# Four low parts of the output weights as a product on ScalarE and a subtraction on GpSimd, with the first 450 words of the order around them

## The chip, the cores and the metric

The kernel runs on one core of one Trainium2 chip. A core has five engines with a queue each: TensorE (PE, matrix products), VectorE (DVE), ScalarE (ACT), GpSimd (POOL) and SyncE (SP, which here only issues DMA transfers). Each engine takes its instructions strictly in the order in which the program holds them, and waits at a semaphore where an operand isn't there yet. The metric is the device time of the whole program in microseconds (us), as the median of several runs; smaller is better.

## The reference, cut to what matters

```python
def _attn_ref(q, k, v):                    # 8 batches, 8 heads, 576 positions, 64 per head
    scores = q @ k.transpose / 8           # masked: a band of 32, or every 4th of a band of 128
    attn = softmax(where(masks, scores, -1e9))
    return attn @ v

def _moe_ref(x, w_in, w_out, g_ln):        # x: 4608 x 512, w_in: 512 x 1024, w_out: 1024 x 512
    h = x @ w_in
    sm = softmax(h)                        # over the 1024 columns
    solu = h * sm
    ln = (solu - mean(solu)) / sqrt(var(solu) + 1e-6) * g_ln
    return ln @ w_out
```

The weights and `g_ln` come as 64-bit floats. The kernel reads their bits and makes 32-bit values of them, and it multiplies `g_ln` into the rows of `w_out`.

## The kernel before

**Attention** works in 32 units (n = 0 to 31; a unit is two heads of one batch). A unit goes through these steps, each a *word* of the program: `q` and `v` load its queries, keys and values (SP); `S` makes its scores in PSUM (PE); from unit 6 on `mask` adds the mask (DVE), before that PE does; `max` (DVE); `sub` (DVE up to unit 5, then POOL); `exp` (ACT); `sum` and `inv` (DVE); `norm` (POOL or DVE, by the table `POOL_NORM`); `turn` transposes (DVE); `V` multiplies by the values into PSUM (PE); `xh` and `xc` copy the result out (ACT), and `xl` forms the part below it (DVE or POOL).

**The second layer** works in 36 tiles of 128 rows. Products are in 32-bit words cut into a high and a low part, three products for one. For tiles 0 to 9 the words `hp hq hr hs` (columns 0 to 511) and `ht hu hv hw` (columns 512 to 1023) each make a quarter of one half of `h`, which is three matmuls; `ha hb hc hd` each make two such quarters. Then come `peak` (DVE), `e` (ACT), `gate` (DVE), `mid` (subtracts the mean; ACT or DVE by the table `ACT_CENTRE`), `var` (ACT, and six short steps on POOL), `forth` and `back` (through DRAM, SP), `trA trB` (DVE), `thA thB` (ACT), `tlA tlB` (POOL or DVE) and `o` (PE, 24 matmuls: the product with `w_out`).

**The weights** are 16 blocks of 128 x 512 (b = 0 to 7 are `w_in`, 8 to 15 are `w_out`). For each block `w` loads it (two DMAs of 256 KB), `field` and `low` cut out its bits (ACT), `sign` its sign (ACT if the block is in `ZERO_SIGN`, else DVE), `join` puts them together (DVE), `hi` writes the high part (ACT) and `lo` the low part. Blocks 8 to 15 take in `g_ln` on the way, in one of two forms:

```python
    def conv_gain(b):                                        # line 917, ACT
        cv[b]["gained"] = True
        nc.scalar.activation(out=cv[b]["mag"], in_=cv[b]["mag"], func=AF.Copy, scale=gain(b))
    def conv_lo(b):                                          # lines 929 to 935
        if b < 8 or "gained" in cv[b]:
            eng = nc.vector if b in DVE_LOW else nc.gpsimd
            eng.tensor_tensor(out=out, in0=mag, in1=high, op=ALU.subtract)
        else:
            nc.vector.scalar_tensor_tensor(out=out, in0=mag, scalar=gain(b), in1=high,
                                           op0=ALU.mult, op1=ALU.subtract)
```

Without the word `gain` both `hi` (line 925) and `lo` (line 933) multiply by `g_ln` themselves, and `lo` is on VectorE. With it `hi` is a plain cast (line 923) and `lo` a plain subtraction (line 931). Before the change only block 13 has the word.

**What sets the order.** The text `OPENING` is a list of some 1,200 words. The kernel goes through it once, from left to right, and each word writes its instructions at the end of its engine's queue; nothing sorts them later. So a word's place decides what it stands behind on its own engine, SP's loads among them, and the semaphores do the rest.

**What is shared.** The eight 2 KB banks of PSUM hold everything PE writes: tiles 0, 2, 4 use banks 0 and 1, the tiles between them banks 2 and 3, the scores of units 0 to 3 lie in banks 2 and 3, those of later units in banks 5 and 6, and `V` writes to parts of banks 4 to 7. The regions of `V` and of later `S` are tracked as overlapping, so a `V` waits for whoever still reads the `S` that stands ahead of it in the list, and the other way round. The weights' 64-bit words lie in seven buffers by the table `SLOTS`; block 7 takes that of block 0, block 10 that of block 3, and so on.

Of the kernel before, what the change touches and what calls it, by code (L numbers as in the profile page):

```python
# [42 lines left out]
POOL_NORM = (0, 1, 2, 4, 5, 6, 7, 8, 10, 11, 12, 15, 18, 21, 22)  # L43
ACT_SCORES = ()
POOL_X = (2, 4, 5, 6, 9)
DVE_LOW = (1, 4, 8, 9, 10, 11, 12, 14, 15)
ACT_CENTRE = (0, 3, 4, 5, 6, 8, 9, 10, 11, 13, 14, 15, 17, 19, 20, 21)
# [3 lines left out]
ZERO_SIGN = (2, 3, 5, 6, 7, 9, 11, 12, 13, 15)  # L51
OPENING = (
# [1044 lines left out]
```

## Time and profile before

| | us |
|---|---|
| median of 3 runs | 479.35 (479.26 to 479.41) |
| the profiled execution's own time | 478.46 |
| its span, first to last instruction | 476.7 |
| PE busy in the span | 455.9 (96%) |
| DVE, ACT, POOL busy | 351.3, 296.3, 274.9 |

The span is that of one execution, the times are those of others: a difference that is worked out on the span's clock is carried over to the median as it is. PE's busy time counts a matmul from its start to its modelled end. Where a row of the profile ends in square brackets, the engine stood idle before the instruction, for so many us, and what follows the arrow ended that.

### The profile page before, as it was taken

The page shows a single profiled execution, that of the slowest core. Times are in us where ns is not written, and L with a number is a line of the kernel's source. Part 1 is how long each engine was busy: PE and PEld are TensorE (multiplying, and loading weights), DVE is VectorE, ACT ScalarE, POOL GpSimd, SP SyncE. Part 2 cuts the span into 40 slices and gives each one's busy share as a digit, 9 for nine tenths or more (in the row PEclk, how much of TensorE's full clock was granted, in tenths as well). Part 3 has the DMA queues.
Part 4 walks back from the last instruction along what each step waited for, and adds up shares of the span by engine and source line. Part 5 has one row for each costly group of instructions (what it writes and reads, how often), then busy time and mean ns, then how long its engine had stood idle before and what let it go on. Part 6 is the DMA issues. An engine that isn't in the chain of part 4 may idle for free.

```text
span 476.7 us, 15670 instructions
## 1 busy us (share of the span) xinstructions
PE 455.9 (96%) x6590; PEld 369.5 (78%) x6590; DVE 351.3 (74%) x640; ACT 296.3 (62%) x502; POOL 274.9 (58%) x340
## 2 busy tenths in 40 slices
PE   2689999999999999999999999999999999999996
PEld 1467777888888888888788888888888888888885
DVE  3878899999989497788698948768584845446472
ACT  4687997754456636644755663647585847667452
POOL 0453666654587797985384434647575755656320
PEclk9999999999999999999999999999999999999999
DMA  8999895758647647665677846564854745453461
GB/s 259 321 325 327 271 285 151 209 183 259 210 133 210 173 142 214 195 208 190 176 217 196 258 133 192 151 224 140 286 151 130 204 139 137 130 154 112 110 194 70
DMA packets 56661, 92.57 MB, mean 194 GB/s; under 512 B 6288, under 2 KB 32400, under 8 KB 56592
## 3 DMA queue, kind: packets, MB, share of 16 engines
q1 hardware_dynamic: 55872, 90.93, 62.7%
q8 instruction: 51, 0.84, 0.7%
q10 hardware_dynamic: 720, 0.66, 0.4%
q14 instruction: 18, 0.15, 0.1%
HBM read 58.53 MB, written 28.31 MB: 182 GB/s over the span
## 4 chain that ended last, share of the span: by engine, by line
PE 50%; DVE 1%; issue 0%; ACT 0%; ACTq 0%; DVEq 0%
PE banks L605 24%; PE banks L834 19%; PE banks L406 3%; PE banks L640 2%; PE banks L321 2%; DVE tl L596 0%; DVE t L510 0%; DVE sm L345 0%; DVE pt L390 0%; DVE t L858 0%; ACT ob L654 0%; DVE mu L521 0%; DVE t L522 0%; ACTq L654 0%; DVEq L345 0%
## 5 line engine op out<-in xcount | busy, mean ns | idle before, releaser
L605 PE MATMUL banks<-w_o,th 128*128 128x512 f32 x544 | 168.9, 391 | 0.0
L605 PEld LDWEIGHTS banks<-w_o,th 128*128 128x128 f32 x544 | 101.3, 188 | 21.6 <-DVE mu L510 0.2
L605 PE MATMUL banks<-w_o,tl 128*128 128x512 f32 x272 | 106.0, 390 | 0.0
L596 POOL TENSOR_TENSOR tl<-t,th 128x512 fp32r<-128x512 f32 x36 | 49.7, 1386 | 35.7 <-ACT th L590 33.8
L858 DVE CUSTOM_DVE_ANT_0 t<-banks,t 128x512 f32<-128x512 f32 x39 | 26.6, 688 | 45.9 <-PE banks L834 40.4
L605 PEld LDWEIGHTS banks<-w_o,tl 128*128 128x128 f32 x272 | 51.0, 188 | 10.9
L590 ACT CAST th<-t 128x512 fp32r<-128x512 f32 x68 | 41.0, 617 | 20.9 <-DVE t L582 15.4
L475 PE MATMUL banks<-w_i,x_hi 128*128 128x512 f32 x160 | 52.3, 409 | 0.8 <-DVE mu L510 0.8
L366 POOL TENSOR_TENSOR sm<-sm,mx 128x576 f32<-128x576 f32 x26 | 32.5, 1254 | 28.5 <-DVE mx L353 28.5
L582 DVE STREAM_TRANSPOSE t<-raw 128x512 f32<-128x512 f32 x68 | 46.0, 693 | 1.7 <-DMA raw<-mid 1.5
L321 PE MATMUL banks<-kt,qt 64*32 64x64 f32 x2304 | 34.2, 235 | 13.7 <-DMA qt<-qT 7.4
L321 PEld LDWEIGHTS banks<-kt,qt 64*32 64x32 f32 x2304 | 27.8, 111 | 23.8 <-issue 13.6
L510 DVE CUSTOM_DVE_ANT_0 t<-t,e 128x1024 f32<-128x1024 f32 x25 | 32.0, 1280 | 15.2 <-ACT e L501 15.1
L406 PEld LDWEIGHTS banks<-pt,vt 32*64 32x64 f32 x2624 | 33.7, 135 | 10.9 <-issue 2.6
L501 ACT ACTIVATE e<-t,nmax 128x1024 f32<-128x1024 f32 x25 | 28.8, 1150 | 20.8 <-DVE nmax L865 20.6
L852 ACT COPY t<-banks 128x512 f32<-128x512 f32 x39 | 22.6, 586 | 30.5 <-PE banks L834 21.2
L526 ACT ACTIVATE e<-t 128x1024 f32<-128x1024 f32 x35 | 37.0, 1058 | 6.0 <-DVE t L522 5.7
L617 ACT ACTIVATE ob<-banks,rstd 128x512 f32<-128x512 f32 x35 | 23.9, 684 | 25.0 <-PE banks L605 15.6
L406 PE MATMUL banks<-pt,vt 32*64 32x64 f32 (+1 forms) x2624 | 37.2, 235 | 2.1 <-ACT x_hi L444 1.0
L519 ACT ACTIVATE t<-t,mu 128x1024 f32<-128x1024 f32 x22 | 25.3, 1152 | 16.7 <-DVE mu L518 11.4
L385 POOL TENSOR_TENSOR sm<-sm,rs 128x576 f32<-128x576 f32 x15 | 18.9, 1259 | 28.5 <-DVE rs L380 27.9
L475 PEld LDWEIGHTS banks<-w_i,x_hi 128*128 128x128 f32 x160 | 29.1, 191 | 7.5 <-DVE mu L510 1.3
(162 smaller groups left out, 959.0 us busy)
## 6 DMA issues: line engine op xcount, KB each, us to landing
mid<-t SPq DMA_DIRECT2D x140, 128.0 KB, 2.6
raw<-mid SPq DMA_DIRECT2D x34, 512.0 KB, 3.8
out<-ob SPq DMA_DIRECT2D x35, 256.0 KB, 3.0
vt<-vw SPq DMA_DIRECT2D x24, 352.0 KB, 4.9
kt<-kT SPq DMA_DIRECT2D x24, 304.0 KB, 4.3
qt<-qT SPq DMA_DIRECT2D x24, 288.0 KB, 4.5
x_hi<-x SPq DMA_DIRECT2D x12, 288.0 KB, 3.8
t<-w_in SPq DMA_DIRECT2D x10, 256.0 KB, 4.6
```

What stands on the lines that cost most here:

```text
L321: nc.tensor.matmul(out=ps[WIN * g : WIN * g + WIN, WQ * s0 : WQ * s0 + WQ], lhsT=qt[D * h : D * h + D, q0 : q0 + WIN], rhs=kt[D * h : D * ...
L366: eng.tensor_tensor(out=st[n]["sm"], in0=st[n]["sm"], in1=wide(mx), op=ALU.subtract)
L406: nc.tensor.matmul(out=ps_x[D * h : D * h + D, r // 2, c0 : c0 + k1 - k0], lhsT=vt[WIN * g : WIN * g + WIN, slot, :], rhs=pt[WIN * g : WIN ...
L475: nc.tensor.matmul(out=ps_h(i)[:, half], lhsT=a[:, kt, xs], rhs=w_i[:, kt, half, part, :], start=(kt == 0 and k == 0), stop=(kt == KT - 1 ...
L501: nc.scalar.activation(out=e, in_=h, func=AF.Exp, bias=nmax, scale=1.0, accum_out=se)
L510: nc.vector.tensor_tensor_reduce(out=t, in0=h, in1=ms[i]["e"], scale=1.0, scalar=0.0, op0=ALU.mult, op1=ALU.add, accum_out=mu,)
L526: nc.scalar.activation(out=e, in_=t, func=AF.Square, accum_out=per_tile(i, "sq"))
L582: nc.vector.transpose(out=turned(i)[:, cut(c)].rearrange("p k (a r) -> p k a r", r=WIN), in_=ms[i]["mv"].rearrange("p (a k s) -> p k a s", ...
L590: nc.scalar.copy(out=ms[i]["th"][:, cut(c)], in_=turned(i)[:, cut(c)])
L596: (nc.gpsimd if on_pool else nc.vector).tensor_tensor(out=ms[i]["tl"][:, cut(c)], in0=turned(i)[:, cut(c)], in1=ms[i]["th"][:, cut(c)].bit ...
L605: nc.tensor.matmul(out=ps_o(i), lhsT=a[:, f, :], rhs=w_o[:, f, part, :], start=(f == 0 and k == 0), stop=(f == FT - 1 and k == 2), skip_gr ...
L834: nc.tensor.matmul(out=banks[:, bank], lhsT=left(pa, kt), rhs=right(pb, kt), start=j in (1, 2, 5) and kt == 0 and k == 0, stop=kt == 1 and ...
```

## The change

Blocks 11, 12, 14 and 15 get the word `gain`, and none of them stands in `DVE_LOW` any more: `g_ln` is multiplied in on ACT, `hi` becomes a cast, and `lo` a subtraction on POOL in place of one VectorE operation. Beside this five tables change, and the first 450 or so words of `OPENING` stand in another order; the rest of it, from `fa1 tlA4 out3 gate7` on, is the same.

```diff
-POOL_NORM = (0, 1, 2, 4, 5, 6, 7, 8, 10, 11, 12, 15, 18, 21, 22)
+POOL_NORM = (0, 1, 4, 5, 6, 7, 10, 11, 12, 15, 18, 21, 22)
-DVE_LOW = (1, 4, 8, 9, 10, 11, 12, 14, 15)
-ACT_CENTRE = (0, 3, 4, 5, 6, 8, 9, 10, 11, 13, 14, 15, 17, 19, 20, 21)
+DVE_LOW = (3, 6, 8, 9, 10)
+ACT_CENTRE = (0, 1, 4, 5, 6, 8, 9, 10, 11, 13, 14, 15, 17, 19, 20, 21)
-ZERO_SIGN = (2, 3, 5, 6, 7, 9, 11, 12, 13, 15)
+ZERO_SIGN = (0, 2, 3, 5, 8, 9, 12, 13, 15)
...
-    "exp3 v2 xl1 w4 ht0 low4 sign4 V2 field4 field6 lo5 hi3 xh2 ht1 xc2 join4 hi4 q5 S5 lo3 w7 "
...
+    "hi3 sub3 exp3 lo2 field6 ht0 lo3 V2 w7 field7 sum3 w10 sign4 xc2 xh2 join6 low7 hq0 inv3 "
+    "norm3 hp1 turn3 field4 sign7 q5 w8 hi6 low10 S5 v3 V3 ht1 join4 hi4 xh3 lo5 q4 lo6 field10 "
...
```

So the low parts of blocks 1 and 4 go from VectorE to POOL and those of 3 and 6 the other way; `norm` of units 2 and 8 goes from POOL to VectorE; `mid` of tile 1 goes from VectorE to ACT and that of tile 3 the other way; of the signs VectorE has seven in place of six and ACT nine in place of ten.

**The loads, on SP's queue, from block 6 on.** `tp` is block 6, `vt_469` (after: `vt_458`) the values of unit 2, `raw` block 4, `kt_537` and `qt_536` (after: `kt_556`, `qt_555`) keys and queries of unit 5, `t<-w_in` block 7, the first `t<-w_out` block 9 (after: 10), the second block 8, and `vt_609` (after: `vt_605`) the values of unit 3. Before:

```order
L258 DMA tp<-w_in 128x512 x2
L258 DMA vt_469<-vw 128x320
L258 DMA vt_469<-vw 128x384
L258 DMA raw_473<-w_in 128x512 x2
L258 DMA kt_537<-kT 128x304 x2
L258 DMA qt_536<-qT 128x288 x2
L258 DMA t_581<-w_in 128x512 x2
L258 DMA t_601<-w_out 128x512 x2
L258 DMA vt_609<-vw 128x320
L258 DMA vt_609<-vw 128x384
L258 DMA t_612<-w_out 128x512 x2
```

And after:

```order
L258 DMA tp<-w_in 128x512 x2
L258 DMA vt_458<-vw 128x320
L258 DMA vt_458<-vw 128x384
L258 DMA raw_467<-w_in 128x512 x2
L258 DMA t_525<-w_in 128x512 x2
L258 DMA t_532<-w_out 128x512 x2
L258 DMA kt_556<-kT 128x304 x2
L258 DMA qt_555<-qT 128x288 x2
L258 DMA t_561<-w_out 128x512 x2
L258 DMA vt_605<-vw 128x320
L258 DMA vt_605<-vw 128x384
```

The queries of unit 5 moved behind two more weight blocks, and the values of unit 3 behind one more.

**VectorE around the softmax of unit 5.** L390 is `turn3`, L353 and L363 on `banks` are `max5` and `sub5`, L461 is `xl3`, L912 a `join`, L931 a `lo`, L904 a `sign`, L374 `sum5`. Before, with the semaphores that each waits for:

```order
L390 STREAM_TRANSPOSE pt_596<-sm_95 128x576 [waits DVE_49]
L353 TENSOR_REDUCE mx<-banks 128x9 [waits PE_49,Activation_49]
L363 TENSOR_TENSOR sm_95<-banks,mx 128x9x64 [waits DVE_49]
L912 SCALAR_TENSOR_TENSOR mag_594<-mag_594,low_585 128x512 [waits Activation_49]
L931 TENSOR_TENSOR w_i<-mag_522,w_i 128x512
L904 TENSOR_SCALAR low_625<-t_612 128x512 [waits DMAHW1_49,DMAHW0_49,Activation_49]
L374 TENSOR_REDUCE rs<-sm_95 128x9 [waits Activation_49]
L461 TENSOR_TENSOR x_lo<-banks,x_hi 128x576 [waits Activation_49]
```

And after:

```order
L390 STREAM_TRANSPOSE pt_550<-sm_95 128x576 [waits DVE_49]
L904 TENSOR_SCALAR low_540<-t_525 128x512 [waits DMAHW7_49,DMAHW6_49,Activation_49]
L912 SCALAR_TENSOR_TENSOR mag_552<-mag_552,low_470 128x512 [waits Activation_49]
L931 TENSOR_TENSOR w_i<-mag_479,w_i 128x512 [waits Activation_49]
L904 TENSOR_SCALAR low_565<-t_532 128x512 [waits DMAHW1_49,DMAHW0_49,Activation_49]
L353 TENSOR_REDUCE mx<-banks 128x9 [waits Activation_49]
L363 TENSOR_TENSOR sm_95<-banks,mx 128x9x64 [waits DVE_49]
L461 TENSOR_TENSOR x_lo<-banks,x_hi 128x576
```

`V3` now stands right behind `S5` in the list and ahead of `max5`. So `V3` no longer waits for `sub5`, and `max5` waits for ACT's count at `xh3`, the copy that follows `V3`.

## Rows read from the trace of the kernel before

**Rows 1.** Busy time by stretch: PE, PEld, DVE, ACT, POOL; then PEclk, DMA, GB/s

```profile
30.00:40.00 10.00, 8.08 (x247) 6.12 (x246) 7.76 (x14) 8.39 (x15) 5.81 (x4) 1.00 0.98 322
30.00:70.00 40.00, 36.20 (x876) 28.05 (x875) 35.83 (x60) 35.48 (x60) 24.34 (x31) 1.00 0.94 297
70.00:220.00 150.00, 150.00 (x2460) 122.47 (x2459) 129.24 (x218) 87.14 (x145) 107.86 (x134) 1.00 0.62 191
```

**Rows 2.** Timeline of PE: start, us, instruction, idle before and its end

```profile
28.15 1.20 PE L406 MATMUL banks<-pt,vt 32*64 32x32 f32 x80
...
31.29 0.79 PE L321 MATMUL banks<-kt,qt 64*32 64x64 f32 x48 [1.05 <-ACT x L448]
32.95 0.43 PE L321 MATMUL banks<-kt,qt 64*32 64x64 f32 x24 [0.86 <-issue]
...
35.73 1.13 PE L406 MATMUL banks<-pt,vt 32*64 32x32 f32 x80
...
55.89 1.13 PE L406 MATMUL banks<-pt,vt 32*64 32x32 f32 x84 [1.01 <-ACT x_hi L444]
...
63.87 0.62 PE L475 MATMUL banks<-w_i,x_hi 128*128 128x512 f32 x2
...
69.27 0.73 PE L475 MATMUL banks<-w_i,x_hi 128*128 128x512 f32 x2 [0.57 <-DVE mu L510]
...
79.82 0.67 PE L605 MATMUL banks<-w_o,th 128*128 128x512 f32 x2
```

**Rows 3.** SP's issues: unit 5's queries, block 9, unit 3's values, each with its landing

```profile
23.88 1.02 SPq L258 DMA_DIRECT2D qt<-qT  x2
...
DMA to landing us min/median/max: 4.6/4.8/4.9
...
26.96 0.97 SPq L258 DMA_DIRECT2D t<-w_out  x2
...
DMA to landing us min/median/max: 4.2/4.8/5.4
...
27.99 0.89 SPq L258 DMA_DIRECT2D vt<-vw  x2
...
DMA to landing us min/median/max: 5.5/5.5/5.6
```

**Rows 4.** Timeline of VectorE, columns as in the timeline of PE

```profile
37.87 0.76 DVE L461 TENSOR_TENSOR x_lo<-banks,x_hi 128x576 fp32r<-128x576 f32 x1 [0.27 <-ACT x_hi L444]
39.62 0.47 DVE L904 TENSOR_SCALAR low<-t 128x512 uint16<-128x512 uint16 x1 [0.99 <-ACT low L891]
...
52.99 0.76 DVE L374 TENSOR_REDUCE rs<-sm 128x9 f32<-128x585 f32 x1 [1.50 <-ACT sm L370]
...
62.22 1.23 DVE L510 CUSTOM_DVE_ANT_0 t<-banks,e 128x1024 f32<-128x1024 f32 x1
...
86.61 0.76 DVE L345 TENSOR_TENSOR sm<-banks,dilated 128x576 f32<-128x576 f32 x1
```

**Rows 5.** Groups by line and form, 0 to 130 us: count, busy, mean ns, idle before

```profile
L385 POOL TENSOR_TENSOR sm<-sm,rs 128x576 f32<-128x576 f32 x11 | 13.8, 1256 | 28.5 <-DVE rs L380 27.9 <-ACT e L501 0.5
L931 POOL TENSOR_TENSOR w_i<-mag,w_i 128x512 fp32r<-128x512 f32 x6 | 7.7, 1297 | 9.1 <-ACT w_i L923 9.1
L933 DVE SCALAR_TENSOR_TENSOR w_o<-mag,packed,w_o 128x512 fp32r<-128x512 f32 x7 | 5.2, 738 | 0.0
L522 DVE TENSOR_SCALAR t<-t,mu 128x1024 f32<-128x1024 f32 x3 | 2.3, 754 | 0.1
L931 POOL TENSOR_TENSOR w_o<-mag,w_o 128x512 fp32r<-128x512 f32 x1 | 1.4, 1417 | 0.0
L919 ACT ACTIVATE mag<-mag,packed 128x512 f32<-128x512 f32 x1 | 0.7, 708 | 0.0
```

**Rows 6.** Timeline of VectorE and of POOL around one `norm`

```profile
40.68 0.64 DVE L912 SCALAR_TENSOR_TENSOR mag<-mag,low 128x512 int32<-128x512 int32 x1
...
40.86 1.49 POOL L385 TENSOR_TENSOR sm<-sm,rs 128x576 f32<-128x576 f32 x1 [2.18 <-DVE rs L380]
```

143 rows, old and new, of the table OPENING are left out of this document.

## The prediction

> **What bounds the kernel now.** I read the busy time by stretch first. From 70 to 220 us PE is busy for 150.00 of 150.00 us, while VectorE is busy for 129.24, ACT for 87.14 and POOL for 107.86 [rows 1]: there no other engine's work can be worth anything, as long as it isn't late. PE stands still ahead of that: between 30 and 70 us it is busy for 36.20 of 40 [rows 1], so 3.8 us are to be had there. The change edits exactly this part, and PE's matmuls are the same before and after. So the question is a single one: at what time does PE begin `o0`, the first product with `w_out` (79.82 now [rows 2]), with the same work behind it? At that point all of units 0 to 10's `S`, units 0 to 7's `V` and all of tiles 0 to 5's `h` are done in both orders, so a shift of `o0` is a shift of the end.
>
> The timeline of PE names the stops: 1.05 us ahead of `S5`, 0.86 inside it, 1.01 ahead of `V5`, 0.57 ahead of `hc5` [rows 2]. VectorE is nearly as full: 35.83 of these 40 us [rows 1], with two stops of its own, 0.99 and 1.50 us [rows 4].
>
> **The low parts themselves.** VectorE loses four fused operations: 4 x 0.738 = 2.95 us [rows 5]. ACT gains four products of 0.708, 2.8 us [rows 5], and POOL four subtractions of 1.297 (`w_i`) to 1.417 (`w_o`), 5.2 to 5.7 us [rows 5]. With the tables beside it: `norm2` and `norm8` put 2 x 0.76 = 1.5 us on VectorE (at the 0.76 of `xl3`, a step of the same size [rows 4]) and take 2 x 1.256 = 2.5 us off POOL [rows 5]; one more sign costs VectorE 0.47 (as the one at 39.62 [rows 4]); `lo1`, `lo4` against `lo3`, `lo6`, and `mid1` against `mid3`, change engines one for one. In sum VectorE does 1.0 us less, POOL 2.7 to 3.2 more, ACT some 2 more. Nothing of this is on PE's path by itself. What hides POOL's share: it is idle for 15.7 of the 40 us from 30 to 70 [rows 1], and the four parts are wanted only from the fourth quarter of `o0` on. Uncovered, it would cost up to the whole 5.7.
>
> **The loads.** SP's queue is issued in order, and the DMA engines are busy for 0.98 of 30 to 40 us at 322 GB/s [rows 1]; so what lands when is a matter of how many bytes stand ahead. Unit 5's second half of queries is issued at 24.57 and lands at 29.2 (24.57 + 4.6 [rows 3]). After, blocks 7 and 10 stand ahead of it: 2 x 524 KB at 322 GB/s are 3.3 us more, so it lands at about 32.5. Unit 3's values land at 34.0 now (28.5 + 5.5 [rows 3]), and stand behind one block more: 34.0 + 1.6 = 35.6; I take 35.5.
>
> **PE up to `V3`.** What stands ahead of `S5` is ready as now: `V2` started at 28.15 [rows 2], and after it come two quarters in place of one, to about 30.7. `S5` then waits for its queries until 32.5 to 33 (31.29 now). The stop of 0.86 in its middle is put down to "issue", time in which PE waits for nothing that the profile shows [rows 2]; I take it as gone, since PE has stood still for 2 us just ahead of it, and as 0.86 at most if not. `S5` ends at about 34, ahead of the values of unit 3 either way, so this does not count. `V3` follows it directly now and starts with those values at 35.5, against 35.73 [rows 2]; it ends at about 36.55 against 36.86. But by then PE has done four quarters (`hp0 ht0 hq0 hp1`) where it had done six. A quarter is three matmuls, 0.69 us from start to start, so PE is 1.4 us of work behind and 0.3 us of time ahead: **1.1 us behind**.
>
> **VectorE from there.** `max5` waits for the copy `xh3` behind `V3`, and everything behind it on VectorE waits too: `sub5`, `xl3`, `join7`, and so on to the `gate` steps. VectorE has run out of work at about 34.8, so it stands still for some 2.4 us. With 0.7 us for the copy (between 0.6 and the 1.0 that lie between the end of `V3` and `xl3` now, 37.87 - 36.86 [rows 2, 4]) `max5` starts at 37.25; it, `sub5` and `xl3` take 2.1 together, to 39.35. Now `xl3` ends at 38.63 and `gate2` at 63.45 [rows 4]: 24.82 us, of which 0.99 and 1.50 are stops, so 22.33 of work. After, the list between the two holds `join7` (0.64), `sum5` (0.76), `sign11` (0.47), `fa0` and `trA0` (at the 0.64 of a `join`) and an `inv` (0.2) more, a sign (0.47) and the VectorE half of `mid1` (0.754 [rows 5]) less: +2.1, or 24.5. I find no stop in it: `exp5`, `exp6`, `e0` to `e2` on ACT and `norm4` to `norm6` on POOL each come ahead of their reader, by 0.1 to 1.5 us. So `gate2` ends at 63.85 and `ha4` starts at 63.95, against 63.87 [rows 2]. The 1.1 us that PE was behind are made up on the way, because the stop of 1.01 ahead of `V5` shrinks to what PE needs to catch up.
>
> **From `ha4` to `o0`** PE's work is the same 15.4 us in both. Now 0.57 of waiting for `gate3` come on top; after, `hc5` stands four quarters later and finds it done. In its place `hb4` waits for `xl7`, which is late by about 0.2. So `o0` starts at 79.82 + 0.1 - 0.57 + 0.2 = 79.55, **0.3 us earlier**. In `o0` the low parts of blocks 11, 12 and 15 are wanted 2, 2.7 and 4.8 us after its start; POOL has them at about 71, 80.5 and 83.3, so the last has 1 us to spare. Behind `o0` stands `V8`, which waits for unit 10's `mask` on VectorE. Its end is 87.37 now [rows 4]; after, VectorE has 1.0 us less to do up to there, 0.7 us of later start, and 2.5 us of stops less, and ends at about 84.6, when `o0` ends at 85.0.
>
> The forecast is therefore 479.35 - 0.3, or **479.0 us** (the execution profiled: 478.46 - 0.3).
>
> **A rule that speaks against it.** The `norm` at 40.86 took 1.49 us [rows 6], where eleven of its kind take 1.256 in the mean [rows 5]. It began inside a VectorE `join`, which reads two operands of SBUF and ended at 41.32, 0.46 us later. The Trainium skill ("SBUF — State Buffer", section "Who interferes with whom") says that a VectorE instruction with two SBUF inputs and a GpSimd instruction that reads SBUF exclude each other on a shared port, and that whichever issues second waits. These rows agree with it. By it the four new subtractions would cost VectorE up to their own length each where they come first, as an estimate 5.7 us at the most; by the row, 0.23 each, 0.9 us in all, and that is spread over both engines. I leave it out of the sum and put it into the second rival.
>
> **Rival 1: the loads come without their pause.** The 1.6 us per block is a mean that holds pauses: the halves of block 9, issued at 26.96 and 27.60, land at 31.2 and 33.0 [rows 3], 1.8 us apart, where 262 KB at the mean rate take 0.8. For it: that pause of 1.0 lies ahead of unit 3's values now, and after it may lie behind them. Against: a share of 0.98 leaves the DMA engines no gap [rows 1], so what makes the pause keeps them busy, and is likely to come again at about this time. Without it `V3`, `max5` and all behind them come about 1.0 to 1.2 earlier: 477.9 us.
>
> **Rival 2, slower: VectorE stands still as much as now.** Place: between `max5` and unit 10's `mask`, a single chain without reserve. For it: the two stops of now, 0.99 and 1.50 [rows 4], have the same kinds of cause (a weight's bits, an `exp` behind POOL's `sub`), several margins above are under 0.3 us, and a collision like that of rows 6 costs 0.23 each time. Against: ACT's and POOL's steps come ahead by my walk. Each microsecond moves `gate2`, `ha4`, `o0` and `V8` by as much. From 1.3 us on the kernel is slower by more than 0.2%; with the full 2.49 it takes 481.5 us.
>
> **Rival 3: PE itself is the bound up to `ha4`.** If the stop called "issue" comes back in another of the dense stretches (`S6` stands three quarters behind `S4` now, five before), PE, which has little to spare after `V3`, loses its 0.9: 479.9 us.
>
> **How the numbers follow.** A measurement of this kernel can tell about 0.2%, 0.96 us, from no change. Forecast (0.45): its own range is 478.0 to 479.9, from 0.6 to 1.0 for the copy and 35.3 to 35.6 for the values; 0.09 of it is faster by over 0.2%, 0.36 within. Rival 1 (0.23): faster. Rival 2 (0.22): slower. Rival 3 (0.10): 0.04 within, 0.06 slower. Faster 0.32, same 0.40, slower 0.28. The range runs from 477.3, below rival 1's 477.9, to 481.3, most of rival 2; some 0.15 lies outside.
>
> **What would show it.** In the profile after: `S5` with an idle of about 2 us put down to the DMA of `qt`; `V3` at about 35.5, waiting for `vt`; VectorE idle for 2.4 us ahead of `max5`, ended by ACT's `x_hi`; then no stop over 0.3 until 85; the 0.57 ahead of `hc5` gone; `o0` near 79.5; 150 of 150 us of PE behind it. Wrong it would be if `V3` starts a microsecond off 35.5, if VectorE has another stop over 0.5, or if `V8`, `S11` or `o0`'s last quarters wait: then the lead is given back after 80 us, where I take PE to be full.

## The result: slower by 1.0%

After takes 483.94 us (median of 8 runs, 481.68 to 486.72), before 479.31 beside it (8 runs, 478.08 to 481.06). The ratio is 1.0102, with an interval of 1.0072 to 1.0132. All ratios here compare means of fast runs; of e2, e3, e6, e14, e17 and e18 one run each, over 1.5% above the kernel's fastest, is left out of them. The forecast was 479.0, and its range ended at 481.3. The profiled execution of after took 484.52 us, with a span of 482.7; its last product begins 6.05 us later than that of before (477.92 against 471.87).

The busy time by stretch, against [rows 1] (columns: stretch, its length, busy us and count of PE, PEld, DVE, ACT and POOL, then PE's granted clock, DMA share, GB/s):

```profile
30.00:40.00 10.00, 9.08 (x247) 7.00 (x248) 7.91 (x14) 8.07 (x15) 2.77 (x2) 0.83 0.94 293
30.00:70.00 40.00, 36.42 (x891) 28.17 (x891) 35.82 (x60) 34.78 (x57) 21.74 (x26) 0.96 0.82 255
70.00:220.00 150.00, 147.80 (x2421) 120.27 (x2422) 127.85 (x211) 86.85 (x147) 108.93 (x138) 1.00 0.66 198
```

From 70 to 220 us PE, full before, now stands still for 2.20 us. PE's timeline at the words of [rows 2] (`S5`, `V3`, `S6`, `V5`, `ha4`, `o0` with its last quarter, `V8`; in brackets the idle time ahead and who ended it):

```profile
33.66 1.53 PE L321 MATMUL banks<-kt,qt 64*32 64x64 f32 x72
...
36.31 1.10 PE L406 MATMUL banks<-pt,vt 32*64 32x32 f32 x80 [0.78 <-DMA vt<-vw]
...
46.63 0.59 PE L321 MATMUL banks<-kt,qt 64*32 64x64 f32 x13 [1.57 <-DMA qt<-qT]
...
60.26 0.99 PE L406 MATMUL banks<-pt,vt 32*64 32x32 f32 x70 [0.98 <-DMA vt<-vw]
...
67.18 0.62 PE L475 MATMUL banks<-w_i,x_hi 128*128 128x512 f32 x2
...
82.98 0.73 PE L605 MATMUL banks<-w_o,th 128*128 128x512 f32 x2 [0.36 <-DVE mu L510]
...
87.87 1.03 PE L605 MATMUL banks<-w_o,th 128*128 128x512 f32 x2
...
89.62 1.13 PE L406 MATMUL banks<-pt,vt 32*64 32x32 f32 x84 [0.49 <-DVE sm L345]
```

`ha4` begins 3.3 us later than before, `o0` 3.2. The pair at 87.87 takes 1.03 in place of 0.62, which is a wait inside it for the last low part, and `V8` waits for unit 10's mask. `S14`, PE's last word ahead of the part that both texts share, begins 4.2 us later than before, and `S16`, two units on, 5.6. So 2.5 us are lost behind `o0`: 1.05 up to `S14`, of which those two waits are 0.9, and 1.4 in the part that both share, where `hc8` waits 0.68 for a `gate` and `S15` has a stop of 0.54 called "issue", time in which PE waits for nothing that the profile shows. After's `S14`, `hc8`, second piece of `S15`, and `S16`:

```profile
123.41 0.97 PE L321 MATMUL banks<-kt,qt 64*32 64x64 f32 x72
...
126.11 0.72 PE L475 MATMUL banks<-w_i,x_hi 128*128 128x512 f32 x2 [0.68 <-DVE mu L510]
...
134.03 0.48 PE L321 MATMUL banks<-kt,qt 64*32 64x64 f32 x33 [0.54 <-issue]
...
144.19 0.97 PE L321 MATMUL banks<-kt,qt 64*32 64x64 f32 x72
```

and `S14` and `S16` before:

```profile
119.20 0.97 PE L321 MATMUL banks<-kt,qt 64*32 64x64 f32 x72
...
138.57 0.97 PE L321 MATMUL banks<-kt,qt 64*32 64x64 f32 x72
```

What the forecast did not see stands in VectorE's timeline (`max5`, `sign11`, `gate2`, `xl7`, tile 3's `mid`, `gate4`, `join15`, `mask10`):

```profile
38.12 0.76 DVE L353 TENSOR_REDUCE mx<-banks 128x9 f32<-128x576 f32 x1 [1.97 <-ACT x_hi L444]
...
49.64 0.48 DVE L904 TENSOR_SCALAR low<-raw 128x512 uint16<-128x512 uint16 x1 [1.23 <-ACT low L891]
...
64.78 1.16 DVE L510 CUSTOM_DVE_ANT_0 t<-banks,e 128x1024 f32<-128x1024 f32 x1
...
71.55 0.76 DVE L461 TENSOR_TENSOR x_lo<-banks,x_hi 128x576 fp32r<-128x576 f32 x1 [0.71 <-ACT x_hi L444]
...
75.76 1.83 DVE L522 TENSOR_SCALAR t<-t,mu 128x1024 f32<-128x1024 f32 x1
...
81.71 1.21 DVE L510 CUSTOM_DVE_ANT_0 t<-banks,e 128x1024 f32<-128x1024 f32 x1
...
84.14 1.33 DVE L912 SCALAR_TENSOR_TENSOR mag<-mag,low 128x512 int32<-128x512 int32 x1
...
88.82 0.74 DVE L345 TENSOR_TENSOR sm<-banks,dilated 128x576 f32<-128x576 f32 x1
```

and in that of GpSimd two of the four new subtractions, the one that stands beside tile 3's `mid`, and that of block 15:

```profile
75.75 1.29 POOL L931 TENSOR_TENSOR w_o<-mag,w_o 128x512 fp32r<-128x512 f32 x1 [1.09 <-ACT w_o L923]
...
86.96 1.38 POOL L931 TENSOR_TENSOR w_o<-mag,w_o 128x512 fp32r<-128x512 f32 x1 [2.04 <-ACT w_o L923]
```

### The profile page after: what moved, and what is told of

It reads as the page before. It is cut to its first block, busy times and chain, and to the rows that moved or that the text cites. A ratio compares the mean times of both kernels' runs of the same rounds, so it can differ in the third digit from the quotient of the medians.

```text
span 482.7 us, 15673 instructions
## 1 busy us (share of the span) xinstructions
PE 458.1 (95%) x6590; PEld 370.3 (77%) x6590; DVE 354.4 (73%) x639; ACT 297.5 (62%) x505; POOL 278.5 (58%) x342
## 4 chain that ended last, share of the span: by engine, by line
PE 50%; DVE 1%; issue 0%; ACT 0%; ACTq 0%; DVEq 0%
PE banks L605 24%; PE banks L834 19%; PE banks L406 3%; PE banks L640 2%; PE banks L321 2%; DVE tl L596 0%; DVE t L510 0%; DVE sm L345 0%; DVE pt L390 0%; DVE t L858 0%; ACT ob L654 0%; DVE mu L521 0%; DVE t L522 0%; ACTq L654 0%; DVEq L345 0%
## 5 line engine op out<-in xcount | busy, mean ns | idle before, releaser
L406 PEld LDWEIGHTS banks<-pt,vt 32*64 32x64 f32 x2624 | 33.8, 135 | 13.3 <-issue 4.3
L834 PE MATMUL banks<-w_i,x_lo 128*128 128x512 f32 x124 | 33.4, 394 | 0.0
```

What stands on the lines that cost most here:

```text
L406: nc.tensor.matmul(out=ps_x[D * h : D * h + D, r // 2, c0 : c0 + k1 - k0], lhsT=vt[WIN * g : WIN * g + WIN, slot, :], rhs=pt[WIN * g : WIN ...
L834: nc.tensor.matmul(out=banks[:, bank], lhsT=left(pa, kt), rhs=right(pb, kt), start=j in (1, 2, 5) and kt == 0 and k == 0, stop=kt == 1 and ...
```

## The experiments

The theories ahead of the runs: the new order, of the loads above all, costs the time (O); the change of engines costs it, by collisions and late low parts (E). Each diff shows the words of `OPENING` that move, or the line that changes. All runs in one table; `ha4` and `S16` are PE's starts of these words in each kernel's one profiled execution (where an expectation says `S14` of such a start, it is that of `S16`).

| | ratio to before | interval | `ha4` | `S16` |
|---|---|---|---|---|
| before | 1 | | 63.87 | 138.57 |
| after | 1.0102 | 1.0072 to 1.0132 | 67.18 | 144.19 |
| e1 engines alone | 1.0039 | 1.0021 to 1.0058 | 64.88 | 141.13 |
| e2 order alone | 1.0118 | 1.0090 to 1.0145 | 68.70 | 148.56 |
| e3 loads sooner | 1.0059 | 1.0033 to 1.0086 | 65.99 | 143.72 |
| e4 quarter sooner | 1.0113 | 1.0078 to 1.0147 | 65.81 | 143.57 |
| e5 engines, placed | 1.0061 | 1.0038 to 1.0084 | 64.72 | 142.95 |
| e6 first loads too | 1.0072 | 1.0043 to 1.0102 | 66.53 | 144.16 |
| e7 thin subtractions | 1.0069 | 1.0043 to 1.0096 | 64.47 | 140.84 |
| e8 max5 ahead | 1.0123 | 1.0090 to 1.0155 | 67.72 | 143.94 |
| e9 old to ha4 | 1.0084 | 1.0053 to 1.0115 | 67.87 | 146.07 |
| e10 new to ha4 | 1.0048 | 1.0027 to 1.0069 | 65.34 | 140.97 |
| e11 old to ha4, fused | 1.0126 | 1.0097 to 1.0154 | 64.28 | 147.26 |
| e12 old to S4 | 1.0103 | 1.0077 to 1.0128 | 67.01 | 144.43 |
| e13 V8 behind o1 | 1.0296 | 1.0251 to 1.0341 | 65.80 | 153.34 |
| e14 mid3 on ACT | 1.0082 | 1.0050 to 1.0114 | 65.47 | 141.95 |
| e15 three together | 1.0265 | 1.0220 to 1.0309 | 65.27 | 152.63 |
| e16 new to ha4, loads | 1.0011 | 0.9988 to 1.0035 | 63.25 | 138.71 |
| e17 loads and mid3 | 1.0051 | 1.0025 to 1.0078 | 65.22 | 142.39 |
| e18 all causes | 1.0064 | 1.0034 to 1.0094 | 64.68 | 142.62 |

The rows of the experiments name lines one or two lower than after's, or one higher in e7, since the word list fills fewer or more lines of text.

**e1 and e2: engines or order?**

```diff
-join14 hi14 hi11
+join14 gain14 hi14 gain11 hi11
...
-hi12
+gain12 hi12
...
-hi15 lo15
+gain15 hi15 lo15
```

> The order of before, with the change of engines alone: each of blocks 11, 12, 14 and 15 gets its gain on ScalarE right ahead of its hi, and its low part is a subtraction on GpSimd. Theory O (the new order, above all of the loads, costs the time; the engines are beside the point): PE stands still ahead of o0 as before, o0 begins at 79.8 give or take 0.3, and the time is that of before within 0.3%, 478.3 to 480.5 us. Theory E (the four subtractions collide with VectorE's operations, or come too late for o0): low parts 12 and 15 hold up the third quarter of o0 or its last by 0.5 us or more, or VectorE's unit-9 and unit-10 steps come 1 us later, and the time is 480.5 to 482.5 us.

In e2 the four `gain` words are taken out of after:

> The order and tables of after without the four gain words: the low parts of blocks 11, 12, 14 and 15 are one VectorE operation again. Theory O: PE's stops for q6 and for v5 (1.57 and 0.98 us in after) and the fallen clock from 31.5 to 34.9 us stay, o0 begins at 82.5 to 83.5, and the time stays at 483 to 485 us. Theory E: what comes behind o0 (the late last quarter of o0, V8 waiting 0.49 us for mask10) goes, some 2.5 us: 481 to 481.8 us.

Engines alone cost 0.39%, order alone 1.18%, so O holds for most of it. E is not nothing: e1's time, 481.46 us, lies in E's range. Both together cost less than the sum, as if in the new order the change of engines helped; the intervals of e2 and after overlap, so this rests on e11 below. e1's price has an address, as I read the rows. Around `xl7` and `sum8` VectorE now stands still twice, and `S10` waits for `mask9` (two rows of VectorE, one of PE):

```profile
73.38 0.76 DVE L460 TENSOR_TENSOR x_lo<-banks,x_hi 128x576 fp32r<-128x576 f32 x1 [1.10 <-ACT x_hi L443]
...
75.86 0.76 DVE L373 TENSOR_REDUCE rs<-sm 128x9 f32<-128x585 f32 x1 [1.07 <-ACT sm L369]
```

```profile
79.28 0.97 PE L320 MATMUL banks<-kt,qt 64*32 64x64 f32 x72 [0.71 <-DVE sm L344]
```

The two gains stand ahead of `xh7` on ScalarE, and two subtractions ahead of `sub8` on GpSimd. VectorE was relieved of two operations here, 1.48 us, and stands still for 2.17.

**e5: the same, with these steps behind what they held up**

```diff
-join14 hi14 hi11 gate3
+join14 gate3
...
-lo14 xh7 q10 xl7 low15
+xh7 q10 xl7 gain14 hi14 gain11 hi11 low15
...
-lo11 sub8 exp8 mid3 sum8 hb4
+sub8 exp8 mid3 sum8 lo11 lo14 hb4
```

> As e1 (the order of before with the change of engines), but the new steps stand behind what they held up there: the gains and high parts of blocks 14 and 11 behind the copy xh7 on ScalarE, their subtractions behind sub8 on GpSimd, low part 13 ahead of tile 3's variance steps, and the gain, high and low part of block 15 ahead of mid4. Theory H (in e1 the cost was where the new steps stood: VectorE waited 1.10 us for x_hi ahead of xl7 and 1.07 us ahead of sum8, so mask9 came 1 us late for S10, and three subtractions in a row ended behind what o0 wanted): both stops of VectorE are under 0.3 us, S10 waits for nothing, and the time is before's, 479.3 to 480.5 us. Rival K (the collisions of a subtraction on GpSimd with VectorE cost wherever it stands): 481 to 482 us, as e1.

Neither theory: `xl7`'s stop shrank to 0.31, but the gains now stand ahead of `exp8`, and `sum8` waits three times as long:

```profile
76.96 0.77 DVE L373 TENSOR_REDUCE rs<-sm 128x9 f32<-128x585 f32 x1 [3.15 <-ACT sm L369]
```

`S10` waits 2.03 for it. The stop moved with the gains: what holds VectorE up there is ScalarE's work ahead of the step that it wants next. Whether collisions cost as well, e5 does not tell.

**e9, e10, e12, e11: which stretch?** These join the two texts at a word: up to it the one, then what is left in the order, tables and engines of the other. e9 takes before up to `ha4`, e10 is its reverse, e12 takes before up to `S4` (40 us), and e11 is e9 without the four `gain` words.

> The order and tables of before up to the word ha4 (64 us), and what is left in the order, tables and engines of after (gains on ScalarE, subtractions on GpSimd). Theory L (the loss lies ahead of ha4, where PE in after is 3.3 us behind before, by its waits for loads): ha4 at 64 and o0 near 80, and the time is that of before within 0.2%, 479 to 480.2 us. Theory B (what lies behind ha4 loses by itself: S14 comes 2.5 us later against o0 in after, by low parts that end late and by unit 10's mask): 481 to 482.3 us.

> The reverse of e9: the order and tables of after up to the word ha4, and what is left in the order, tables and engines of before (low parts 11, 12, 14 and 15 one operation on VectorE). Theory L: PE is some 3 us behind at ha4 as in after, and that stays: 482 to 483 us. Theory B: 480 to 481.3 us, since the part behind ha4 is that of before; less than the full 3.3 us may be left of PE's lag, if PE has waits to give up there (the 0.57 us for gate3).

> The order and tables of before up to the word S4 (40 us), the order, tables and engines of after behind it. Against after this tells what the first 40 us lose, against e9 what lies from S4 to ha4. Theory L with the loss at the start (q5, v3 and the first loads, the wait of max5 for the copy behind V3): within 0.5 us of e9. Theory L with the loss at q6, block 11 and v5 (PE's 1.57 and 0.98 us, VectorE's 1.23 us for block 11): 1.5 to 2.5 us above e9, at 482.5 to 484 us.

> As e9, without the four gain words: behind ha4 the order of after, but the four low parts are one operation on VectorE. Against e9 this tells what the change of engines by itself is worth in the new order. Theory E (the subtractions on GpSimd cost, by late low parts and by collisions with VectorE): 1 us or more faster than e9. Rival W (VectorE is the engine that is late behind ha4, and 2.95 us of work more on it cost more than the collisions): 1 to 2 us slower than e9, with o0 waiting for gate4.

The part behind `ha4` costs 0.84% by itself (e9), the part ahead of it 0.48% (e10): B holds, and a smaller L beside it. e12 is no better than after, so what is lost ahead is lost behind `S4`, as far as these intervals tell (those of e12 and e9 overlap too). e11 is Rival W: with the fused operations VectorE is so late that `o0` and `V8` wait far longer than in after:

```profile
83.75 0.72 PE L604 MATMUL banks<-w_o,th 128*128 128x512 f32 x2 [2.29 <-DVE mu L509]
...
91.23 1.13 PE L405 MATMUL banks<-pt,vt 32*64 32x32 f32 x84 [1.57 <-DVE sm L344]
```

So in the new order the change of engines wins some 0.4% (the intervals of e9 and e11 just overlap); the order needs it, and loses more than that by itself.

**e3, e16, e6: the loads ahead of ha4**

```diff
-V2 w7 field7 sum3 w10
+V2 q5 w7 field7 sum3 w10
...
-q5 w8 hi6 low10 S5 v3 V3
+v3 w8 hi6 low10 S5 V3
...
-w9 hu0 hv0 max5 sub5 low8 sign8 v7 q6
+q6 w9 hu0 hv0 max5 sub5 low8 sign8 v7
...
-w12
+v5 w12
```

> After, with four small loads put ahead of the weight blocks they stood behind: q5 ahead of blocks 7 and 10, v3 ahead of block 8, q6 ahead of block 9, v5 ahead of block 12. Theory O, the loads' part of it: q6 lands by about 45 in place of 46.8 and v5 by 58 in place of 60.1, PE's waits of 0.78 (V3), 1.57 (S6) and 0.98 (V5) us go, and o0 begins 2 to 3 us sooner, at 80 to 81: 481 to 482 us. Rival V (VectorE's chain is the limit all the same, since gate2 ended at 64.8 in after): ha4 cannot begin ahead of 65, o0 gains 1 at most: 483 us. Theory E: no change, 484 us.

e16 is the same edit in e10; e6 adds `q2` ahead of `w0` to e3.

> As e10 (the order of after up to ha4, that of before with the fused low parts behind it: 1.0048), with the loads of e3, q5, v3, q6 and v5 sooner. Theory L (the loads are the loss ahead of ha4): 1.000 to 1.003, 479.5 to 481 us, V3 without its wait for v3. Rival (the rest of the new order ahead of ha4, such as max5 behind the copy xh3 and VectorE's four more steps, or the first loads): it stays at 1.004 to 1.006.

> As e3 (after, with q5, v3, q6 and v5 sooner), and q2 ahead of block 0 as well, as it stood before. Theory O (the loads' order costs it, at the start too): S2's stops of 3.1 us for q2 become 1.6 as in before, V2 comes 1 to 1.5 us sooner, and the ratio to before falls by some 0.2 to 0.3% from e3's 1.006: about 481 to 481.7 us. Rival (something else is late right behind, block 0 for hp0 or PE's stops called issue): the ratio stays at 1.006, 482.5 to 483 us.

e3 and e16 each win some 0.4%, and e16 is level with before. In e16 `V3` waits for nothing, and `o0` begins 0.2 us from where it did before:

```profile
34.08 1.12 PE L404 MATMUL banks<-pt,vt 32*64 32x32 f32 x80
...
80.01 0.62 PE L603 MATMUL banks<-w_o,th 128*128 128x512 f32 x2
```

So the four loads are most of the loss ahead of `ha4`, as far as the intervals tell: those of e10 and e16 overlap by 0.08%. Which of the four binds was not tried, and e12 does not fit easily: there `q5`, `v3` and `q6` stand where before has them, PE's profile names no wait for a load between 22 us and `ha4`, and it costs as much as after. e3's ratio lies between theory O's and rival V's; `S6` has its queries in time there, but is stopped by "issue" instead, for 0.79 us in e3, 0.91 in e6 and 0.76 in e16. e6 shows no gain over e3, and the rival holds for the first loads.

**e4 and e8: other suspects ahead of ha4**

```diff
-V2
...
-hq0
+hq0 V2
```

> After, with one quarter of h (hq0, three matmuls) put ahead of V2, so that PE has dense work while it waits there. Theory C (the fall of PE's granted clock to half, from 31.5 to 34.9 us in after, is what costs and what makes the times spread, and it comes of the thin work ahead of it): the clock stays at full, PE's quarter takes 0.7 in place of 1.05 us, V3 and all behind it come 1 to 1.5 us sooner, and the time is 482.5 to 483 us with a spread under 2 us. Theory O: the loads set the pace behind V3 anyway (v3 at 36.2, q6 at 46.8, v5 at 60.1), and the time stays within 0.5 us of 483.9.

```diff
-V3
...
-max5 sub5
+max5 sub5 V3
```

> After, with max5 and sub5 ahead of V3 in the list again, as before: VectorE no longer waits for the copy behind V3, and V3 waits for sub5. Rival V (VectorE's chain from max5 on is what sets ha4 and o0, as predicted): VectorE's stop of 1.97 us ahead of max5 goes, gate2 and o0 come 1.5 to 2 us sooner: 482 to 482.5 us. Theory P (PE is the one that is late up to ha4, by its waits for v3, q6 and v5): the same waits stay, and the time is 483.5 to 484.5 us.

Neither helps. In e4 `S5` then waited 1.06 and 1.40 us for `q5`, and the clock was granted at 0.66 over 30 to 40 us, against 0.83 in after: the edit moved the thin stretch and did not fill it, so what the clock costs is left open. In e8 VectorE's stop ahead of `max5` fell to 0.93, but `V3` waits for `sub5` in its place:

```profile
36.06 1.59 PE L405 MATMUL banks<-pt,vt 32*64 32x32 f32 x79 [1.64 <-DVE sm L362]
```

**e7 and e14: the subtractions, and the one collision ahead of gate4.** e7 leaves out all but 32 of 512 columns of the four subtractions, and GpSimd writes zeros to the other columns at the program's start; e14 takes `mid3` back to ScalarE.

```diff
-eng.tensor_tensor(out=out, in0=mag, in1=high, op=ALU.subtract)
+c = slice(0, 32) if b in (11, 12, 14, 15) else slice(0, 512)
+eng.tensor_tensor(out=out[:, c], in0=mag[:, c], in1=high[:, c], op=ALU.subtract)
```

> After, with the four new subtractions cut to 32 of 512 columns (the other columns of these low parts are zeros that GpSimd writes at the program's start, so that part of the product is left out); the gains on ScalarE stay. Theory E (the subtractions themselves cost what is lost behind o0): VectorE's steps beside them go back to their usual length (0.75 where 1.83 us stood), the last quarter of o0 and V8 no longer wait, and 1 to 1.5 us are won: 482.4 to 483 us. Theory O: VectorE and the loads are as late without them, and the time stays at 483.5 to 484.5 us.

```diff
-ACT_CENTRE = (0, 1, 4, 5, 6, 8, 9, 10, 11, 13, 14, 15, 17, 19, 20, 21)
+ACT_CENTRE = (0, 1, 3, 4, 5, 6, 8, 9, 10, 11, 13, 14, 15, 17, 19, 20, 21)
```

> After, with tile 3's subtraction of the mean on ScalarE, as in before, in place of VectorE, where it stood beside a subtraction on GpSimd (1.83 us in place of 0.75). Theory X (VectorE's chain to gate4 and mask10 is what o0 and V8 wait for, and the collision is the largest single piece of it): VectorE is 1.8 us ahead at gate4, the stops of 0.36 at o0 and 0.49 at V8 go, and so far as PE can follow 0.8 to 1.3 us are won: ratio 1.0075 to 1.0085, 482.6 to 483.1 us. Rival Y (ScalarE's chain to the high parts of blocks 12 and 15 and to exp8 comes 1.15 us later by it, and o0's later quarters wait longer): no gain, 1.010.

e7 wins 0.33%, e14 0.20% (their intervals and after's overlap, so the rows have to carry it). In e7 the same `mid3` takes 0.78 in place of 1.83, and `V8` follows `o0` without a wait:

```profile
73.95 0.78 DVE L523 TENSOR_SCALAR t<-t,mu 128x1024 f32<-128x1024 f32 x1
```

```profile
86.40 1.13 PE L407 MATMUL banks<-pt,vt 32*64 32x32 f32 x84
```

In e9, where the order behind `ha4` is that of after, `mid3` beside the same subtraction takes 1.78. In e14 `o0` and `V8` wait for nothing either, but now `S11` does, 1.09 us for its queries: the next thing in line.

**e13 and e15: `V8` behind `o1`**

```diff
-o0 V8 v10
+o0 v10
...
-o1
+o1 V8
```

> After, with V8 behind o1 in place of right behind o0, as in before. Theory D (V8 wants unit 10's mask as soon as o0 ends, and VectorE has it 0.5 us late, in all runs with the new order behind ha4): the wait of 0.48 us at V8 goes, nothing comes in its place, and the time is 483 to 483.6 us (ratio 1.008 to 1.009). Rival: V8's result is wanted by ha6 through xh8 and xl8, or unit 10's bank by S11, and the wait comes back there: no change, 1.010.

> After, with the loads of e3 (q5, v3, q6, v5 sooner), V8 behind o1 as in e13 and tile 3's subtraction of the mean on ScalarE as in e14. If loads and VectorE's chain are the two causes, and each hides a part of the other: the ratio is 1.002 to 1.005, 480.5 to 482 us. If the new order has a third cost (PE's stops called issue, which fall elsewhere in each order): 1.006 or more.

Both are 2.6 to 3% slower than before, which neither theory had. A wait did come back at `S11`, as the rival said (2.53 us in e13), but not for unit 10's bank: unit 11's queries were issued at 84.94 and landed 5.2 us later, at 90.1, when unit 10's mask had been done for 2 us. What makes both so slow is a load. The edit left `v10` behind `o0`, and `v10` goes into the buffer that `V8` reads, so SP's queue stood for 10.5 us until `V8` was done; in after `v10` is issued at 90.78. Behind it stands `back4`, issued at 101.64 where after has it at 92.83 (SP, `v10` and `back4`):

```profile
99.32 0.35 SPq L257 DMA_DIRECT2D vt<-vw  x1
...
101.64 0.33 SPq L567 DMA_DIRECT2D raw<-mid  x1
```

VectorE waits for `V8` ahead of `mask11`, which stands behind it in the list, and then 7.56 us for what `back4` brings; `S12` stands for 5.62 us:

```profile
99.33 0.76 DVE L344 TENSOR_TENSOR sm<-banks,dilated 128x576 f32<-128x576 f32 x1 [2.93 <-PE banks L405]
...
107.65 0.71 DVE L581 STREAM_TRANSPOSE t<-raw 128x512 f32<-128x512 f32 x1 [7.56 <-DMA mid<-t]
```

```profile
110.58 1.34 PE L320 MATMUL banks<-kt,qt 64*32 64x64 f32 x72 [5.62 <-DMA out<-ob]
```

In before `S11` and `V8` stand behind both `o0` and `o1`, at 90.87 and 91.77, when unit 10's mask (from 86.61 on [rows 4]) is long there, and `v10` stands far behind them. So e13 does not tell whether `V8`'s own wait could have been moved, and e15, which held this edit, told nothing of the loads and `mid3`.

**e17 and e18: do the causes add up?** e17 is e3 with `mid3` on ScalarE, e18 also has e7's thin subtractions.

> After, with the loads of e3 (q5, v3, q6, v5 sooner) and tile 3's subtraction of the mean on ScalarE as in e14. If the two causes add: 1.0102 less 0.0043 less 0.002, a ratio of 1.003 to 1.005. If VectorE's chain is the one bound behind both (the loads only fill waits that the chain has anyway): 1.006 to 1.008.

> As e17, and the four new subtractions cut to 32 of 512 columns as in e7 (the other columns are zeros, so part of the product is left out). If loads, collision and subtractions are the whole of the loss: 0.999 to 1.002. If the order behind ha4 has a further cost of its own (V8 and gate4 close behind VectorE, PE's stops called issue): 1.003 to 1.006.

Not in full. e17's interval holds the sum of its two causes, 1.004, and its rival as well; e18's lies above the 0.999 to 1.002 that it would have if the three were all. Both keep 0.5 to 0.6%, which is what e18's expectation calls a further cost of the order. The two profiles share a stop, `S11` (e17, then e18):

```profile
89.86 0.96 PE L320 MATMUL banks<-kt,qt 64*32 64x64 f32 x72 [1.39 <-DMA qt<-qT]
```

```profile
88.66 0.96 PE L322 MATMUL banks<-kt,qt 64*32 64x64 f32 x72 [1.41 <-DMA qt<-qT]
```

SP's queue in after shows where this comes from (issues; L560 is a `forth`, L568 a `back`, L258 a load):

```profile
77.62 4.80 SPq L560 DMA_DIRECT2D mid<-t  x8
82.46 0.44 SPq L258 DMA_DIRECT2D vt<-vw  x1
84.58 0.34 SPq L568 DMA_DIRECT2D raw<-mid  x1
85.01 0.38 SPq L258 DMA_DIRECT2D kt<-kT  x1
85.44 1.18 SPq L258 DMA_DIRECT2D qt<-qT  x1
```

The queries of unit 11 (`kt` and `qt` at 85) stand behind `back2`, which waits until `forth2` has landed, and `forth2` stands behind `forth3`, which waits for tile 3's `mid`: that ends at 77.59, and the eight issues begin at 77.62. Before, `q11` stands ahead of `back2`, is issued at 79 and lands at 85.5; in after it lands at 90.1. In after, e7, e17 and e18 it lands 12.5 to 13.3 us behind the first of these issues. So `S11` has a bound that hangs on `mid3` and does not move with what PE wins.

It is not the whole of the 0.5%. In e7 the issues begin at 74.76, `q11` lands at 87.5 and `S11` follows `V8` without a wait, and e7 still costs 0.69%:

```profile
87.65 0.96 PE L322 MATMUL banks<-kt,qt 64*32 64x64 f32 x72
```

And e18 has a longer stop, by "issue" inside `S15`, which stands in the part that both texts share:

```profile
132.41 0.54 PE L322 MATMUL banks<-kt,qt 64*32 64x64 f32 x34 [1.65 <-issue]
```

Ten of the fifteen profiles with the order of after behind `ha4` have such a stop in `S15`, of 0.53 to 1.65 us; none of the five with the order of before there has one over 0.3. What makes it was not followed, and `q11` was not moved in any run.

## Why the prediction was wrong, step by step

- **The low parts themselves.** Their lengths were right: 1.29 to 1.38 on GpSimd. That GpSimd's idle time hides them was wrong. They were to end at 80.5 (block 12) and 83.3 (block 15), and ended at 84.9 and 88.3. Block 15's was so late because its `join` on VectorE began at 84.14 only, and ScalarE's gain and cast come in between. The last pair of `o0` waited 0.4 us for it.
- **The loads.** `v3` was to start `V3` at 35.5; it landed at 36.2, and `V3` began at 36.31. `q5` landed at 33.9, not 32.5, and yet `S5`'s wait of 2 us did not come, since PE was behind by itself: `V2` had stops of 0.18 and, by "issue", 0.97 us ahead of and inside it, and then the granted clock was 0.50, the lower of its two levels (1.2 GHz), from 31.5 to 34.9 us, with pairs of matmuls of 0.91 and 1.05 where 0.62 is usual. The step that failed is what I did not do: I followed `q5` and `v3` through SP's queue and stopped there. `q6`, issued 1.9 us later than before though no more blocks stand ahead of it, took 6.0 us to land in place of 4.1 to 4.8 and made `S6` wait 1.57; block 11 made `sign11` wait 1.23 on VectorE; `v5`, now behind block 14 and `forth0` too, made `V5` wait 0.98; `q11` came 4.6 us later. e3 and e16, which move `q5`, `v3`, `q6` and `v5`, put these four at 0.4%.
- **VectorE from max5 on.** The stop of 2.4 ahead of `max5` was measured as 1.97, and it began at 38.12, not 37.25. "I find no stop in it" is the sentence that fell: 0.87 of later start and 1.23 at `sign11` make `gate2` end at 65.9 in place of 63.85 (a third stop, 0.44, is made up by shorter steps). But `ha4` did not wait for `gate2`, which ended 1.2 us ahead of it: PE stood nowhere between `V5` at 60.26 and `ha4`. So the path was wrong too. What set `ha4` was PE's own lateness, and the 1.1 us were not made up at `V5`, since the stop there did not shrink: 0.98, now for `v5`.
- **From ha4 to o0, and V8.** Predicted 63.95, 79.55 and no wait; measured 67.18, 82.98 and 0.49. `mask10` ended at 89.56, not 84.6, and these make up 4.7 of the 5.0: the 2.1 above, 0.71 ahead of `xl7`, whose copy waited for PE's late `V7`, 0.20 ahead of `gate3`, 1.08 of collision in `mid3`, some 0.65 in `join15`.
- **The collision.** This term was left out of the sum and priced at 0.23 each, from one row of a `norm`. The subtraction on GpSimd at 75.75 began 0.01 us ahead of `mid3` on VectorE, and `mid3` took 1.83 in place of the 0.75 of [rows 5]; `join15`, which began inside the one at 83.64, took 1.33 where joins take 0.64 to 0.68. So it is three to five times dearer than priced, and it should have stood in the sum: the `norm` had overlapped its `join` by 0.46 us only, where these overlap by 1.28 and 0.79. The Trainium skill ("SBUF — State Buffer", section "Who interferes with whom") says that whoever issues first has the shared pair for its whole length, and the other stands still; the trace agrees, up to the last 0.2 us of the 1.29. The same section counts `tensor_scalar`, which `mid3` is, among the operations that can take the pair with one operand from SBUF: I had looked for operations with two alone, and so passed over `mid3`.
- **Where PE is full.** "150 of 150 behind it" became 147.80: I took PE's lead behind `o0` as safe because PE was full there before. As I read the rows, it was full because `V8` stood behind 11 us of `o0` and `o1`; no run shows this by itself, since e13 held up `v10` with it.
- **The rivals.** Rival 2, VectorE standing still as much as now between `max5` and unit 10's mask, is a part of what happened: its stops there add up to 2.58 us, against the rival's 2.49, and the 0.22 was too small. Its 481.5 was too low as well, for it held VectorE's stops, and collisions at 0.23 each, but not the loads that PE waits for. Rival 1 did not occur. Rival 3 did not in after's `S6`, whose stop was for a load, but the stop called "issue" came back inside `V2`, and in e3, e6 and e16 inside `S6` as well.
- **The forecast's own range.** 478.0 to 479.9 is wider than what it names: 0.6 to 1.0 for the copy and 35.3 to 35.6 for the values give 478.7 to 479.4.

e1 against before says that the named edit by itself costs 0.39%, e11 against e9 that it saves 0.4% in the new order. The forecast had both at nothing.

**What stays open.** What the last 0.5% are made of, of which `q11` and the stops called "issue" are parts; which of the four loads binds, and why e12 is no faster; what the half clock costs; and how much of a single profile is chance, of which more below.

## What to carry to other kernels

When an order changes, follow every load whose place in the queue moved up to the point where the texts meet again, not only the first that bind; a small operand behind a transfer that itself waits (`q11` behind `back2`, and in e13 `back4` behind `v10`) is a bound that no engine's timeline shows until the others are gone. An engine that is full before says nothing of how it stands when words behind it are moved: ask of each word what it needs and when that comes in the new order. Work taken off a busy engine and put on two others is paid for at whatever stands behind it in their queues (e1, e5), and by whatever of VectorE's runs beside them.

## What the runs showed of the hardware

Kernels that hold the same words up to a point can reach it 4 us apart. Up to `ha4` before, e1, e5, e9 and e11 hold the same words, and PE began `ha4` at 63.87, 64.88, 64.72, 67.87 and 64.28 (mean 65.1) in their profiled executions. With after's first part and its loads it was 67.18, 68.70, 64.47, 65.34, 65.80 and 65.47 (mean 66.2; after, e2, e7, e10, e13, e14), with the loads of e3 65.99, 65.27, 63.25, 65.22 and 64.68 (mean 64.9; e3, e15 to e18). The means lie 1.0 and 1.3 us apart, but the values of one group spread over 2.7 to 4.2. So these profiles do not tell how much of the 3.3 us between before and after at `ha4` is loss and how much is spread from profile to profile (that of e9 is itself 3 us slower than e9's median); of the times, e10 puts after's first part at 0.48%, 2.3 us. The transfers differ from run to run as well: in e1, whose text is that of before up to there, block 4 was issued 0.5 us later than in before and landed 2 to 2.5 us later, and `S5` waited 2.42 where it had waited 1.05. A difference of a microsecond between two profiles is no evidence by itself; the medians and what a row names are.
